# Splitting two GpSimd sums of the second half of the features, the first part ahead of the second matrix

## The chip, the cores and the metric

One core of one Trainium2 chip. The metric is the device time in microseconds of one execution of the whole program, median of several runs. The core's engines, as the profile names them: PE (TensorE, matrix products), PEld (its weight loads), DVE (VectorE), ACT (ScalarE), POOL (GpSimd), SP (SyncE, which issues most DMAs). Each engine works through its own queue of instructions in order; they wait for each other by semaphores.

## The reference

```python
# attention: batch 8, 8 heads, 576 positions, 64 wide; only the 32 best keys of a row count
scores = scale * np.matmul(q, k.transpose(0, 1, 3, 2))
kth = np.partition(scores, -32, axis=-1)[..., -32:-31]
scores = np.where(scores >= kth, scores, -1e9)
attn = softmax(scores)                    # in short
x = np.matmul(attn, v)                    # -> (4608, 512)
# feed-forward: 512 -> 2048 -> 512
h = x @ w_in
g = h - np.tanh(h)
out = g @ w_out
```

The softmax is written out in the reference, with the maximum of the row taken off and 1e-9 added to the sum.

## The kernel before

**Steps of attention.** A step is 128 rows of queries for one pair of heads (144 steps). Per step PE computes the scores (L350) into PSUM, ACT copies them out (L358), VectorE finds the 32nd largest value per row (L380 to L403: maxima of pairs, MAX8, match and replace), POOL makes from it a bias `tb` (L417) and `nb` (L426), ACT and POOL form the masked scores `z` (ACT L436, then POOL L439) and a check flag `bad` (POOL L443, for the step's two heads), ACT takes the exponential (L459), POOL adds the epsilon to its sum `rd` (L469), VectorE inverts it (L478), ACT multiplies (L485), VectorE transposes (L517), a DMA round trip sorts the blocks, and PE multiplies with the values (L582). Several steps are under way at once; in one round of the loop POOL gets, in this order, the z and flags of the last step, then `tb` and `nb` of the present one, then `rd` of the last.

**Feed-forward in units.** When 256 rows of x are complete they form a full unit (17 of them; two smaller units of 128 rows come first). A full unit is a list of 30 items of work, which are dealt out between the steps at a rate that a planner sets when the program is built. So the order on every engine is fixed in the program.

Items 0 to 15 (`ffn_full`, which calls `ffn_h`) form the features g = h - tanh(h), 128 of the 2048 features to an item. On every odd item ACT computes the tanh (L652) and copies h (L653), and POOL subtracts (L654). The features lie in two tiles `u.g[0]` and `u.g[1]`, "the first half" and "the second half" (index k), of four parts m = 0 to 3, each written by one odd item: items 9, 11, 13 and 15 write parts 0 to 3 of the second half.

Items of the product (`ffn_p`, 0 to 13) multiply g with the second matrix `w_out`. This is not done plainly but in Strassen's manner with seven products (`ORDER`), each in two items, k = 0 and 1. The tile of each half is split into four quarters, a11, a12, a21, a22 (`quarters`; in memory they lie in alternating blocks of 128 columns). The seven products take as left sides a11, a12, S2, S3, S1, a22 and S4, in this order, where the sums are, from `sum_up`:

- S1 = a21 + a22, into a buffer of its own (`sums[k]`, in the tile that the profile calls `et`)
- S3 = a21 - a11, in place of a21
- S2 = S1 - a11, in place of a11
- S4 = a12 - S2 (a11's place), in place of a12

POOL computes all of them, at L727, eight for each full unit. In the program each is put behind an item's matrix products. For the first half, S1 and S3 come in items 8 and 9 of the features. For the rest a table says behind which item of the product they come (first the half k, then the sum):

```python
SUMS = {
    0: [(1, "S1")],
    1: [(0, "S2"), (1, "S3")],
    2: [(1, "S2")],
    3: [(0, "S4")],
    4: [(1, "S4")],
}
```

PE's product items 0 and 1 read a11, items 2 and 3 a12, items 4 and 5 S2 of the first and second half, 6 and 7 S3, 8 and 9 S1, 10 and 11 a22, 12 and 13 S4. S2 may overwrite a11 once items 0 and 1 are through and S3 is formed. All of these products are at L626; `hx` and `hy` are the two accumulators. In the profile S2's products are the ones with `hx<-more,g` (first half) and `hx<-et,g` (second half), since their right sides lie in tiles of those names. The results are copied out by ACT (L786 to L803) and joined by POOL (L774).

Of the kernel before, what the change touches and what calls it, by code (L numbers as in the profile page):

```python
# [54 lines left out]
def kernel(  # L55
# [9 lines left out]
    nc = tc.nc  # L65
# [6 lines left out]
    S2 = S // 2  # L72
# [557 lines left out]
    def ffn_h(u, item):  # L630

        w = u.n
        per = 2 * P // w
        for f in range(item * per, (item + 1) * per):
            j, fo = f // FJ, (f % FJ) * P
            s = f * w % 512
            if s == 0:
                cur[u] = next_h("hps")
            for c in range(CD):
                (nc.tensor.matmul if per > 1 else by_columns)(  # L640
                    cur[u][:, s : s + w],
                    w_in[j][:, c, fo : fo + P],
                    u.xT[:, c, 0:w],
                    start=(c == 0),
                    stop=(c == CD - 1),
                )
        if item % 2:
            th = thpool.tile([P, 512], FP32, tag="th", name="th")
            if item % 8 == 1:
                u.g.append(gpool.tile([P, 4, 512], FP32, tag="g", name="g"))  # L650
            g = u.g[-1][:, item % 8 // 2, :]
            nc.scalar.activation(th[:], cur[u][:], AF.Tanh)  # L652
            nc.scalar.copy(g, cur[u][:])  # L653
            nc.gpsimd.tensor_tensor(g, g, th[:], ALU.subtract)  # L654
# [57 lines left out]
    def quarters(u, k):  # L712

        x = u.g[k][:].rearrange("p m (f t n) -> p m f t n", f=2, t=2)
        return [[x[:, :, f, t, :] for f in range(2)] for t in range(2)]

    def sum_up(u, k, x):

        (a11, a12), (a21, a22) = quarters(u, k)
        s1 = sums[k]  # L720
        out_, a, b, op = {
            "S1": (s1, a21, a22, ALU.add),
            "S3": (a21, a21, a11, ALU.subtract),
            "S2": (a11, s1, a11, ALU.subtract),
            "S4": (a12, a12, a11, ALU.subtract),
        }[x]
        nc.gpsimd.tensor_tensor(out_, a, b, op)  # L727

    ORDER = [("A11", "B11"), ("A12", "B21"), ("S2", "T2"), ("S3", "T3"), ("S1", "T1"), ("A22", "T4"), ("S4", "B22")]
    def bring(x):  # L730
# [4 lines left out]
    def product(u, i, k):  # L735
# [18 lines left out]
        return acc  # L754

    SUMS = {
        0: [(1, "S1")],
        1: [(0, "S2"), (1, "S3")],
        2: [(1, "S2")],
        3: [(0, "S4")],  # L760
        4: [(1, "S4")],
# [2 lines left out]
    def ffn_p(u, item):  # L764
# [11 lines left out]
        for x in SUMS.get(item, []):  # L776
            sum_up(u, *x)
# [32 lines left out]
    def combine_next():  # L810

        if combined[0] < len(COMBINE):
            x, j = COMBINE[combined[0]]
            if now[0] < (17 if x == "T3" else 20 if x in ("T2", "T4") else 0):
                return
            combine(x, j)
            combined[0] += 1
# [7 lines left out]
    def ffn_full(u, item):  # L825

        ffn_h(u, item)
        combine_next()
        if item in (8, 9):
            sum_up(u, 0, ("S1", "S3")[item - 8])  # L830

    def ffn(u):

        nh = CF * u.n // (2 * P)
        full = len(u.blocks) == 2
        for item in range(nh):
            f = (item + 1) * CF // nh - 1
            yield CD * (f // FJ + 1), u, lambda item=item: (ffn_full if full else ffn_h)(u, item)
        if not full:
            for part in range(CF // 2):  # L840
                yield CD * (WJ + part // 2 + 1), None, lambda part=part: ffn_small_o(u, part)
            return
        for item in range(2 * len(ORDER)):
            yield 2 * WJ * CD, None, lambda item=item: ffn_p(u, item)
# [277 lines left out]
```

## Time and profile before

| | us |
|---|---|
| median of 3 runs | 1488.9 (1487.57 to 1489.81) |
| the profiled execution | 1492.79 |
| its span, first to last instruction | 1489.7 |
| mean granted clock of PE | 0.971 |

The profile comes from one execution, and its instructions cover the span; about 3.1 us of that execution lie outside it.

| group (line, engine) | count | busy us | mean ns |
|---|---|---|---|
| sums L727 POOL, 128x512 | 136 | 174.4 | 1282 |
| differences g L654 POOL, 128x512 | 144 | 184.6 | 1282 |
| masked scores z L439 POOL, 128x576 | 288 | 405.3 | 1430 |
| joins L774 POOL, 128x256 | 51 | 37.4 | 734 |
| products with w_in L626 PE (`hps`) | 3840 | 438.9 | 384 |
| products with w_out L626 PE (`hx`, `hy`) | 2176 | 256.1 | 385 |

"Busy" is the time an engine had an instruction of that group under way; the 136 sums are the profile's three groups of that line added up. In 50 us stretches between 300 and 1250 us VectorE is busy for 47.6 to 49.9 us and PE for 45.1 to 50.0; from 1350 us on VectorE has almost nothing left to do and PE works off the remaining units.

### The profile page before, as it was taken

The page shows a single profiled execution, that of the slowest core. Times are in us where ns is not written, and L with a number is a line of the kernel's source. Part 1 is how long each engine was busy: PE and PEld are TensorE (multiplying, and loading weights), DVE is VectorE, ACT ScalarE, POOL GpSimd, SP SyncE. Part 2 cuts the span into 40 slices and gives each one's busy share as a digit, 9 for nine tenths or more (in the row PEclk, how much of TensorE's full clock was granted, in tenths as well). Part 3 has the DMA queues.
Part 4 walks back from the last instruction along what each step waited for, and adds up shares of the span by engine and source line. Part 5 has one row for each costly group of instructions (what it writes and reads, how often), then busy time and mean ns, then how long its engine had stood idle before and what let it go on. Part 6 is the DMA issues. An engine that isn't in the chain of part 4 may idle for free.

```text
span 1489.7 us, 35143 instructions
## 1 busy us (share of the span) xinstructions
PE 1378.2 (93%) x12036; PEld 881.8 (59%) x12036; DVE 1284.1 (86%) x4906; ACT 1031.8 (69%) x1922; POOL 1106.4 (74%) x1573
## 2 busy tenths in 40 slices
PE   4667899889999899999999999999999999999998
PEld 2455565556665555656666666666665666656665
DVE  7998988999999999999999999999999999883000
ACT  4776687778787777777687777777777777664321
POOL 3777679968788786968696969696978796866523
PEclk9787999999999999999999999999999999999999
DMA  9954101776776676676766767667666666643311
GB/s 258 359 206 169 55 21 64 187 198 164 194 181 185 162 189 176 173 191 153 180 152 192 177 175 183 182 162 195 167 179 176 170 163 190 155 129 110 105 32 46
DMA packets 241084, 242.25 MB, mean 163 GB/s; under 512 B 177408, under 2 KB 185600, under 8 KB 233728
## 3 DMA queue, kind: packets, MB, share of 16 engines
q1 hardware_dynamic: 239120, 239.69, 59.6%
q8 instruction: 98, 1.61, 0.5%
q14 instruction: 90, 0.74, 0.2%
q10 hardware_dynamic: 1776, 0.22, 0.1%
HBM read 153.99 MB, written 85.85 MB: 161 GB/s over the span
## 4 chain that ended last, share of the span: by engine, by line
PE 56%; DVE 25%; POOL 8%; DMA 5%; ACT 3%; issue 2%; SPq 1%; DVEq 0%; ACTq 0%; POOLq 0%
PE hps L626 23%; PE hx L626 10%; PE hy L626 7%; PE scps L350 6%; PE av L582 6%; DVE m L400 4%; DVE top L392 3%; DVE zx L517 3%; DVE rest L403 3%; POOL z L439 2%; POOL g L727 2%; DVE ab L386 2%; DVE top L403 1%; DVE ab L381 1%; PE hps L640 1%
## 5 line engine op out<-in xcount | busy, mean ns | idle before, releaser
L439 POOL TENSOR_TENSOR z<-sc,z 128x576 f32<-128x576 f32 x288 | 405.3, 1430 | 66.6 <-ACT z L436 66.2
L626 PE MATMUL hps<-xT,w_in 128*64 128x256 f32 x3840 | 438.9, 384 | 3.7 <-ACT g L653 3.6
L626 PEld LDWEIGHTS hps<-xT,w_in 128*64 128x64 f32 x3840 | 270.8, 138 | 162.9 <-issue 26.0
L654 POOL TENSOR_TENSOR g<-g,th 128x512 f32<-128x512 f32 x144 | 184.6, 1282 | 111.6 <-ACT g L653 110.3
L485 ACT ACTIVATE z<-z,rd 128x576 f32<-128x576 f32 x252 | 181.0, 766 | 80.4 <-DVE rd L478 78.5
L459 ACT ACTIVATE z<-z,nb 128x576 f32<-128x576 f32 x288 | 221.9, 775 | 16.5 <-POOL z L439 16.4
L436 ACT ACTIVATE z<-sc,tb 128x576 f32<-128x576 f32 x288 | 208.2, 775 | 27.6 <-POOL tb L417 23.9
L392 DVE MAX8 top<-ab 128x8 f32<-128x144 f32 x864 | 194.7, 295 | 0.0
L358 ACT COPY sc<-scps 128x1152 f32<-128x1152 f32 x144 | 160.9, 1118 | 47.8 <-PE scps L350 47.1
L517 DVE STREAM_TRANSPOSE zx<-z 128x1152 f32<-128x1152 f32 x126 | 171.6, 1362 | 24.1 <-ACT z L485 18.3
L350 PE MATMUL scps<-kT,qT 64*128 64x288 f32 (+1 forms) x1120 | 160.3, 435 | 28.4 <-DVE top L388 26.1
L400 DVE MAX8 m<-rest 128x8 f32<-128x168 f32 x576 | 161.6, 322 | 0.0
L400 DVE MAX8 m<-top 128x8 f32<-128x144 f32 (+1 forms) x576 | 152.8, 307 | 0.0
L350 PEld LDWEIGHTS scps<-kT,qT 64*128 64x128 f32 (+1 forms) x1120 | 87.4, 179 | 86.4 <-ACT z L436 26.6
L652 ACT ACTIVATE th<-hps 128x512 f32<-128x512 f32 x144 | 84.6, 587 | 75.3 <-PE hps L626 68.4
L626 PE MATMUL hx<-w_out,g 128*64 128x256 f32 x1088 | 130.7, 389 | 1.9 <-POOL g L654 1.9
L626 PE MATMUL hy<-more,g 128*64 128x256 f32 x1088 | 125.4, 381 | 0.0
L386 DVE TENSOR_TENSOR ab<-scps,sc 128x576 f32<-128x576 f32 x144 | 107.7, 748 | 0.0
L417 POOL TENSOR_SCALAR tb<-m 128x1 f32<-128x1 f32 x288 | 84.7, 304 | 29.7 <-DVE m L400 28.9
L626 PEld LDWEIGHTS hx<-w_out,g 128*64 128x64 f32 x1088 | 77.1, 139 | 48.8 <-issue 5.1
L626 PEld LDWEIGHTS hy<-more,g 128*64 128x64 f32 x1088 | 76.7, 137 | 43.0 <-issue 5.6
L443 POOL TENSOR_SCALAR bad<-top,tb 128x3 uint8<-128x3 f32 x288 | 97.5, 347 | 0.1
(126 smaller groups left out, 2350.9 us busy)
## 6 DMA issues: line engine op xcount, KB each, us to landing
there<-zx SPq DMA_DIRECT2D x56, 1152.0 KB, 4.9
spare<-there SPq DMA_DIRECT2D x224, 288.0 KB, 5.4
more<-kept_T SPq DMA_DIRECT2D x34, 512.0 KB, 3.8
out_dram<-ot SPq DMA_DIRECT2D x32, 256.0 KB, 2.9
there<-zx SPq DMA_DIRECT2D x14, 576.0 KB, 7.1
spare<-there SPq DMA_DIRECT2D x56, 144.0 KB, 3.2
vb<-in_v_dram SPq DMA_DIRECT2D x48, 128.0 KB, 5.4
kin<-in_k_dram SPq DMA_DIRECT2D x84, 72.0 KB, 4.4
```

The source lines that it names most:

```text
L350: nc.tensor.matmul(ps[rows, t, s, 0:S2], qT[g.b, g.hp + i, g.part][half(t), qs], kT[g.b, g.hp + i][half(t), ks], start=True, stop=True,)
L358: nc.scalar.copy(sc[:], ps[:, :, :, 0:S2])
L386: nc.vector.tensor_tensor(low[:, :, :, 0:W2], thirds(near), thirds(far), ALU.min)
L392: nc.vector.max(top[:, t, o : o + 8], low[:, t, i, :])
L400: nc.vector.max(m[:, t, m8], seen[i][t])
L436: nc.scalar.activation(zv[:, t, :], scf[:, t, :], AF.Relu, bias=tb[:, t : t + 1], scale=-BIG)
L439: nc.gpsimd.tensor_tensor(zv[:, t, :], scf[:, t, :], zv[:, t, :], ALU.subtract)
L459: nc.scalar.activation(x["zv"][:, t, :], x["zv"][:, t, :], AF.Exp, bias=x["nb"][:, t : t + 1], scale=scale, accum_out=den[:, t : t + 1],)
L485: nc.scalar.activation(x, x, AF.Copy, scale=rds[n][:, g.i, t : t + 1])
L517: nc.vector.transpose(tiles(zx, g.nq)[:, :, :, g.i, :].rearrange("p c k j -> p k c j"), z[:].rearrange("p (k c j) -> p k c j", c=NG, j=G),)
L626: nc.tensor.matmul(acc[half(t)], lhs[:, half(t)], rhs, start=start, stop=stop, skip_group_check=True)
L654: nc.gpsimd.tensor_tensor(g, g, th[:], ALU.subtract)
```

## The change

S1 and S3 of the second half are each formed in two instructions in place of one. `sum_up` gets an argument `ms`, the parts m that it covers. Parts 0 and 1 are summed behind items 12 and 13 of the features: S1 behind item 12 and S3 behind item 13, when items 9 and 11 have written those parts. Parts 2 and 3 are summed where the whole sum stood. All other sums stay whole and where they are.

```diff
-    def sum_up(u, k, x):
+    def sum_up(u, k, x, ms=slice(0, 4)):
...
-        nc.gpsimd.tensor_tensor(out_, a, b, op)
+        nc.gpsimd.tensor_tensor(out_[:, ms], a[:, ms], b[:, ms], op)
...
     SUMS = {
-        0: [(1, "S1")],
-        1: [(0, "S2"), (1, "S3")],
+        0: [(1, "S1", slice(2, 4))],
+        1: [(0, "S2"), (1, "S3", slice(2, 4))],
         2: [(1, "S2")],
         3: [(0, "S4")],
         4: [(1, "S4")],
...
         if item in (8, 9):
             sum_up(u, 0, ("S1", "S3")[item - 8])
+        if item in (12, 13):
+            sum_up(u, 1, ("S1", "S3")[item - 12], slice(0, 2))
```

The order of the instructions differs on POOL alone; on PE, VectorE, ACT and SP it is the same in both programs.

## The prediction

> **What bounds the kernel now.** I read four views, in this order: the busy times and the chain that ended last on the page, the groups of GpSimd's instructions kept apart by shape, the view of the sums' line with who waits for it, and then the timeline of each engine around all 17 full units.
>
> ```profile
> PE 1378.2 (93%) x12036; PEld 881.8 (59%) x12036; DVE 1284.1 (86%) x4906; ACT 1031.8 (69%) x1922; POOL 1106.4 (74%) x1573
> ...
> PE 56%; DVE 25%; POOL 8%; DMA 5%; ACT 3%; issue 2%; SPq 1%; DVEq 0%; ACTq 0%; POOLq 0%
> ```
>
> TensorE (PE) and VectorE (DVE) take turns as the bound; POOL is 74% busy and holds 8% of the chain. So a POOL instruction matters only where somebody stands waiting for it. Who waits for the sums is in the view of their line:
>
> ```profile
> who waited for it (us, times):
>   PEld hx L626: 13.6, 13
>   PE hx L626: 7.8, 8
> ```
>
> PE stands 7.8 us in all (its weight loads 13.6, in which the usual gap of some 0.4 before a load after another kind of matmul is included). What the queue looks like at such a place, here the unit at 705 us, first POOL and then PE:
>
> ```profile
> 692.53 0.23 POOL L469 TENSOR_SCALAR rd<-den 128x2 f32<-128x2 f32 x1 [0.66 <-ACT z L459]
> 694.56 1.29 POOL L654 TENSOR_TENSOR g<-g,th 128x512 f32<-128x512 f32 x1 [1.81 <-ACT g L653]
> ...
> 699.19 1.28 POOL L727 TENSOR_TENSOR et<-g 128x512 f32<-128x512 f32 x1
> 700.44 1.28 POOL L727 TENSOR_TENSOR g<-et,g 128x512 f32<-128x512 f32 x1
> 701.67 1.28 POOL L727 TENSOR_TENSOR g<-g 128x512 f32<-128x512 f32 x1
> 702.94 0.58 POOL L417 TENSOR_SCALAR tb<-m 128x1 f32<-128x1 f32 x2
> 703.49 0.25 POOL L426 TENSOR_SCALAR nb<-m 128x2 f32<-128x2 f32 x1
> 703.82 0.23 POOL L469 TENSOR_SCALAR rd<-den 128x2 f32<-128x2 f32 x1
> 704.13 1.28 POOL L727 TENSOR_TENSOR g<-et,g 128x512 f32<-128x512 f32 x1
> ```
>
> ```profile
> 705.46 1.95 PE L626 MATMUL hx<-et,g 128*64 128x256 f32 x16 [1.75 <-POOL g L727]
> ```
>
> The L727 rows are, in order, S1 of the second half, S2 of the first, S3 of the second and S2 of the second. The last is what PE waits for; S1 and S3 of the second half stand ahead of it, though PE wants S3 two product items later and S1 four. Ahead of 694.56 POOL had idled for 0.66 and 1.81 us. The queue is also late for others: VectorE's reciprocal and, through the flags' L443, its row L388 wait for POOL at
>
> ```profile
> 464.48 0.17 DVE L478 RECIPROCAL rd<-rd 128x2 f32<-128x2 f32 x1 [0.48 <-POOL rd L469]
> ...
> 633.05 0.17 DVE L478 RECIPROCAL rd<-rd 128x2 f32<-128x2 f32 x1 [0.47 <-POOL rd L469]
> ...
> 1218.38 0.45 DVE L388 TENSOR_TENSOR top<-ab,scps 128x288 f32<-128x288 f32 x1 [0.95 <-POOL bad L443]
> ```
>
> **What the Trainium skill says.** "GPSIMD Engine Reference", section 2.1, puts a dispatch cost on every instruction and a two-input floor of about 2.5 cycles an element. The trace agrees in form: 456 ns for 128x128 (L600), 734 for 128x256 (L774), 1282 for 128x512, which is 275 ns for each 128 columns and some 180 fixed; splitting a sum pays the fixed part twice. "Perfetto Trace Analysis", section "GPSIMD Engine Instruction", wants spacings of starts rather than durations; here 1.24 between sums against 1.28 reported, and 0.69 after L774. "SBUF — State Buffer", section "SBUF: two separate sides", has GpSimd and VectorE block each other on shared ports; the 136 sums take 1268 to 1312 ns whatever VectorE does, so I put no price on that. "Perfetto Trace Analysis", section "Optimization Strategy", says to find the gaps of the bounding engine and what ends them, which is what the sum below does.
>
> **The change part by part.**
>
> *Added:* per full unit two half sums: S1's after item 12, S3's after item 13. Each costs 0.70 us of queue (L774's shape, same bytes; the strided full-size rows cost no more than the contiguous ones, 1283 against 1280, so bounds of 0.65 and 0.75). *Removed:* half of S1 at product item 0 and of S3 at item 1: 1.24 - 0.70 = 0.54 each. Net on POOL: 2 x (0.70 - 0.54) = 0.32 a unit, x 17 = 5.4 us of 1106. No DMA, no queue of SP or ACT and no matmul moves. The order of POOL around the new pieces, as the two programs have it: L654 of item 11, half S1, [z, flags of the step], L654 of 13, half S3, [tb, nb, rd], L654 of 15; where a step boundary falls differs from unit to unit. Neither half waits for another engine: what each reads was written by POOL's own L654 before.
>
> *What the added halves delay.* I walked POOL's queue through each unit: later by 0.70 at each new half, less each idle gap, minus 0.54 at each shortened sum. The delay on the way peaks at 1.3 to 1.4 just after the second half. Behind it are L654 of items 13 and 15 (PE's first product), z (L439; ACT's exponential waits), tb (ACT's mask) and rd (VectorE's reciprocal). Cover, from the consumers' starts in the trace: rd has 1.4 to 4.2 us of slack against at most 1.3; z 0.67 at the tightest against 0.70; tb 1.2 to 4.4 against 1.4, with the exception of the unit at 1062 (0.19), where ACT then idles 2.56 us before its next instruction, so 1.2 is swallowed there. L654 of item 15 mostly waits for ACT after idle gaps of 0.56 to 2.19. In the units at 773 and 846 it does not, and arrives 1.32 late at 773.2 and 845.6; PE wants this last quarter some 3.2 us into the product, at 773.5 and 846.3. So I price the delays at 0, with 0.3 at each of these two as the other bound, and 2 us in all if the cover of tb and z is thinner than it looks.
>
> *What the shortened sums advance.* At the first half's S2 POOL is 0.54 earlier, less delay left; from the second half's S2 on 1.08, less delay left. By the walk the advance there is 1.05 to 1.08 in the units around 378, 455, 543, 624, 705, 1067, 1212 and 1285, 0.94 at 1142, 0.54 at 782, and 0.4 to 0.75 at 850, 922 and 994. What that is worth is the smaller of advance and wait, where the wait is on the chain:
> - 464.5: reciprocal 0.48.
> - 624 to 633: reciprocal twice 0.47, together 0.94.
> - 705: PE waits 1.75, so 1.08; VectorE, next on the chain, idles 2.16 for these scores.
> - 782: PE waits 1.58, advance 0.54.
> - 1142: PE waits 1.47, advance 0.94.
> - 1218: L388 waits 0.95 behind POOL's flags, and PE's scores 1.83 behind L388: 0.95.
> - 1282 and 1285: PE waits 0.29 and 0.65: 0.94.
>
> Together 5.87 us. Worth nothing: the unit at 543 (PE waits 1.75, but VectorE and DMA carry the chain there until 570, where PE waits for VectorE again), those at 295, 378, 850, 922, 994 and 1067 (PE or VectorE busy throughout) and the three in the last 150 us, where PE is the bound and waits for none of the sums. From this I take 1.0: dependent neighbours on POOL show gaps of 0.08, and with two more such neighbours a unit the advance is some 0.15 smaller at seven places. Result: 4.9 us.
>
> Against the profiled execution: 1492.8 (span 1489.7 and 3.1 around it) - 4.9 = 1487.9. The median shown is 3.9 below that execution, so the forecast for it is 1488.9 - 4.9 = 1484.0. What would be late next: at 705 and 1142 PE still waits 0.5 to 0.7 for the same S2, at 782 1.0; at the other places VectorE or PE itself.
>
> **The rivals.**
> - *The time goes into another wait.* PE and VectorE alternate, and VectorE is at 95 to 100% in most of the 50 us stretches from 300 to 1250; what PE gains at 705, 782 or 1142 it could spend at its next scores, waiting for L388, as it does at 570. For it: 26.1 us of such waits in 12 places. Against: after 782 PE runs 190 us without a break, after 1142 67 us, while VectorE idles. If only those two and 1285 hold half their value: 1.2 us, so 1487.7.
> - *The extra pieces come at the wrong place: slower.* The place is items 12 to 15, where tb, rd and L654 stand behind up to 1.4 us of new work. It decides once POOL's idle gap before item 15's L654 is gone, as at 773 and 846 already: then PE's product waits about 0.7 (1.4 less half of it in the ACT wait) in 12 of the 14 units ahead of the tail, 8.4 us, against which the gains above still count for 4: 1493.3. For it: two units without a gap, tb slacks of 1.2 and less. Against: 12 of the 14 have a gap of 0.56 and more, seven of them over 1.
> - *It doesn't do what it says.* If the tracking of overlaps made PE's first product wait for the half S3 (interleaved columns of the same tile), that half would still precede item 15's L654 in POOL's order, for which PE waits anyway: no time, and the kinds of waits on PE are the same in both programs. I give this no chance of its own.
>
> **How the numbers follow.** Forecast, 1482 to 1485.9: 0.57. Still better by luck of the new alignment, about 1480: 0.03. Time moved to other waits, 1486 to 1491.8: 0.27. Slower, 1492 to 1496: 0.13. A measurement here can tell about 0.2% (3 us) from nothing; so faster 0.60, same 0.27, slower 0.13. Range with 2 in 10 left out: 1481.5 to 1490.5; the forecast's own is 1482 to 1485.9.
>
> **What would show it.** Rows of L727 with 128x256, 68 of them near 0.73 us, POOL busier by some 5 us; PE's waits for L727 down from 7.8 to about 3; the 0.47 and 0.48 waits of the reciprocal gone; no new waits of PE for L654 (1.9 us now) or of ACT for tb (23.9). Wrong if these waits shrink while PE's waits for L388 (26.1) grow as much, or if L654's grow.

## The result and the profile after

| | before | after |
|---|---|---|
| median of 6 runs each, us | 1489.4 (1487.6 to 1490.6) | 1482.9 (1481.0 to 1484.6) |
| ratio after to before | | 0.9955 (0.9945 to 0.9965) |
| the profiled execution / its span, us | 1492.8 / 1489.7 | 1481.0 / 1479.2 |

The change takes off 6.5 us, between 5.2 and 8.2 by the interval. The forecast was a gain of 4.9 us and a time of 1484.0.

A part of the 6.5 us lies outside the profile. In the kernel before, some 3.3 us of an execution lie outside the span of its instructions (3.1 in the profiled one); in the kernel after it is 1.8, and so it is in every kernel of the experiments below, also in those that gain nothing. These 1.4 us are thus not the work of the earlier sums. Where they come from is open. Between the first and the last instruction the change takes off some 5 us.

The busy times and the chain that ended last, from the page of the kernel after:

```profile
PE 1371.2 (93%) x12036; PEld 876.7 (59%) x12036; DVE 1281.5 (87%) x4906; ACT 1030.9 (70%) x1922; POOL 1113.0 (75%) x1607
...
PE 44%; DVE 35%; POOL 9%; DMA 5%; ACT 4%; issue 2%; SPq 1%; DVEq 0%; ACTq 0%; POOLq 0%
```

POOL has 34 instructions more and is busy 6.6 us longer (1106.4 before). The shares of the chain are not a verdict: a second profile of the same kernel gave PE 52%, DVE 29%, POOL 6%. PE and VectorE are so close to each other that small shifts pass the chain from one to the other.

GpSimd's groups of line 727 in the kernel after, shapes kept apart (busy us, mean ns of one, then the idle time of POOL just before them):

```profile
L727 POOL TENSOR_TENSOR g<-g 128x256 f32<-128x256 f32 x34 | 25.0, 736 | 0.0
L727 POOL TENSOR_TENSOR et<-g 128x256 f32<-128x256 f32 x34 | 25.0, 735 | 1.7
```

68 half sums of 0.735 us. Who waits for that line, in the kernel after:

```profile
who waited for it (us, times):
  PEld hx L626: 7.4, 9
  PE hx L626: 3.8, 4
```

PE stood 7.8 us for the sums before, and stands 3.8 now. The view of all waits of the kernel after (total us, times, longest) has the other queues that the prediction spoke of:

```profile
PE scps L350 <- DVE top L388: 29.8, 14, 5.3
...
ACT z L436 <- POOL tb L417: 20.0, 15, 3.6
...
ACT z L459 <- POOL z L439: 12.9, 21, 2.2
...
DVE rd L478 <- POOL rd L469: 8.3, 4, 3.1
```

VectorE's wait for `rd` went from 12.9 to 8.3 us, ACT's for `tb` from 23.9 to 20.0 and for `z` from 16.4 to 12.9: these three came no later in sum. PE's wait for the last part of the second half's features (L654) grew from 1.9 to 2.5, and that of its weight loads from 3.7 to 5.8; growth there was one of the prediction's signs of being wrong. The kernel of the ten other units below has 2.6 and 5.6 and is no slower for it, so no time can be seen in it. PE's wait for VectorE's L388 is 3.7 us longer here than before, which the prediction had named as the sign of a rival. In the second profile of the change it is 25.5, below the 26.1 of before: it varies with the execution and says nothing on the change.

The unit that the prediction had shown, now at 696. First POOL, then PE (start, duration, engine and line, in brackets the idle time before and its releaser):

```profile
683.03 1.27 POOL L654 TENSOR_TENSOR g<-g,th 128x512 f32<-128x512 f32 x1
684.27 0.73 POOL L727 TENSOR_TENSOR g<-g 128x256 f32<-128x256 f32 x1
684.99 0.58 POOL L417 TENSOR_SCALAR tb<-m 128x1 f32<-128x1 f32 x2
...
686.17 1.29 POOL L654 TENSOR_TENSOR g<-g,th 128x512 f32<-128x512 f32 x1
...
690.80 0.73 POOL L727 TENSOR_TENSOR et<-g 128x256 f32<-128x256 f32 x1
691.49 1.28 POOL L727 TENSOR_TENSOR g<-et,g 128x512 f32<-128x512 f32 x1
692.74 0.73 POOL L727 TENSOR_TENSOR g<-g 128x256 f32<-128x256 f32 x1
...
694.64 1.27 POOL L727 TENSOR_TENSOR g<-et,g 128x512 f32<-128x512 f32 x1
```

```profile
695.97 1.95 PE L626 MATMUL hx<-et,g 128*64 128x256 f32 x16 [1.04 <-POOL g L727]
```

Before, POOL idled for 0.66 and 1.81 us ahead of the last L654; now neither idle gap is there, and that time holds the half sums. From 690.80 the three sums ahead of `tb` take 2.66 us up to 693.46, where they had taken 3.75 before (699.19 to 702.94). PE's wait is 1.04 in place of 1.75.

**How much of the two profiles' difference is the change's.** The spans differ by 10.5 us, but 3.8 of these are there at 250 us, before the first full unit. And PE's granted clock falls to half for 3.4 or 6.8 us now and then (a dip, below), and not at all the same places in each execution. Stretches of the kernel after (PE busy, number of matmuls, granted clock, DMA share, GB/s):

```profile
1310.00:1315.00 5.00, 2.67 (x24) 0.95 0.00 0
1315.00:1320.00 5.00, 5.00 (x32) 0.71 0.58 239
```

and the same work in the kernel before:

```profile
1322.00:1327.00 5.00, 2.67 (x26) 1.00 0.00 0
1327.00:1332.00 5.00, 5.00 (x44) 1.00 0.58 236
```

The dip at 1314 costs the kernel after 1.6 us. So a ledger, the gain listed place by place, is only to be had between two executions whose dips lie alike; the experiments gave such a pair.

### The profile page after: what moved, and what is told of

Same layout as the page of the kernel before. It is cut to its first block, busy times and chain, and to the rows that moved or that the text cites. A ratio compares the mean times of both kernels' runs of the same rounds, so it can differ in the third digit from the quotient of the medians.

```text
span 1479.2 us, 35177 instructions
## 1 busy us (share of the span) xinstructions
PE 1371.2 (93%) x12036; PEld 876.7 (59%) x12036; DVE 1281.5 (87%) x4906; ACT 1030.9 (70%) x1922; POOL 1113.0 (75%) x1607
## 4 chain that ended last, share of the span: by engine, by line
PE 44%; DVE 35%; POOL 9%; DMA 5%; ACT 4%; issue 2%; SPq 1%; DVEq 0%; ACTq 0%; POOLq 0%
PE hps L626 17%; PE hx L626 8%; PE hy L626 6%; DVE m L400 6%; PE scps L350 5%; PE av L582 5%; DVE top L392 5%; DVE zx L517 4%; DVE rest L403 4%; DVE ab L386 3%; POOL z L439 3%; DVE top L403 2%; DVE ab L381 2%; POOL g L654 2%; DVE scps L380 2%
## 5 line engine op out<-in xcount | busy, mean ns | idle before, releaser
L654 POOL TENSOR_TENSOR g<-g,th 128x512 f32<-128x512 f32 x144 | 184.5, 1282 | 93.6 <-ACT g L653 91.8
L459 ACT ACTIVATE z<-z,nb 128x576 f32<-128x576 f32 x288 | 222.0, 777 | 13.0 <-POOL z L439 12.9
L358 ACT COPY sc<-scps 128x1152 f32<-128x1152 f32 x144 | 161.1, 1118 | 49.9 <-PE scps L350 49.4
```

The source lines that it names most:

```text
L358: nc.scalar.copy(sc[:], ps[:, :, :, 0:S2])
L459: nc.scalar.activation(x["zv"][:, t, :], x["zv"][:, t, :], AF.Exp, bias=x["nb"][:, t : t + 1], scale=scale, accum_out=den[:, t : t + 1],)
```

## The experiments

The theory of the prediction: the gain arises at seven places, where somebody waits for POOL on the chain, as large as the smaller of wait and advance there; the added pieces cost nothing, since they lie in idle gaps of POOL. Against it stand that the gain is spread over all units or comes from a new alignment of the whole schedule, and that short pieces help as such, wherever they stand. Each ratio below is to the kernel before, run on the same chip; 0.1% is 1.5 us. Each also holds the 1.4 us from outside the instructions, so a kernel that changes nothing inside them comes out near 0.999. The diffs are against the kernel after.

**Only the seven units, and only the other ten.** Units are counted from 0; those at 464, 624, 705, 782, 1142, 1218 and 1285 us are 2, 4, 5, 6, 11, 12 and 13. In the other units the sums stay whole and late. The diff is that of the seven; the second kernel has `AHEAD = (0, 1, 3, 7, 8, 9, 10, 14, 15, 16)`.

```diff
+    AHEAD = (2, 4, 5, 6, 11, 12, 13)
...
-            sum_up(u, *x)
+            sum_up(u, *(x if u.no in AHEAD else x[:2]))
...
-        if item in (12, 13):
+        if item in (12, 13) and u.no in AHEAD:
```

> The early halves are made only in the seven full units (of 17, counted from 0: 2, 4, 5, 6, 11, 12, 13) in which the forecast found somebody waiting on the chain; in the other ten both sums stay whole. Theory 1 (an earlier S2 is worth time only where PE or VectorE stand waiting for GpSimd's queue): the whole gain of the change, 5 to 7 us less than before, ratio 0.9953 to 0.9967. Theory 2 (each unit's burst is eased by about the same, 6.5 us over 17 units): 7/17 of it, 2.7 us, ratio 0.998. Theory 3 (two shorter instructions fit the queue better, wherever they stand): as theory 2, about 2.7 us.

> The early halves are made only in the other ten full units (0, 1, 3, 7, 8, 9, 10, 14, 15, 16). Theory 1: nothing, within 1.5 us of before, ratio 0.999 to 1.001. Theories 2 and 3: 10/17 of 6.5 us, 3.8 us less, ratio 0.9975.

Measured: the seven 1481.8, ratio 0.9944 (0.993 to 0.9959); the other ten 1488.8, ratio 0.9993 (0.9985 to 1.0002). By the medians of the spans alone the seven are 6.7 us shorter than before (1480.0 against 1486.7) and the ten 0.3 longer (1487.0). So the gain inside the instructions arises in the seven units that were picked from the trace of before, and ten times the same two pieces elsewhere are worth nothing and cost nothing that can be measured. The 8.3 us of the seven by the ratio (6.1 to 10.4) lie above the 5 to 7 that were expected; whether they beat the whole change (5.2 to 8.2) is not told apart.

**Both parts at the old place.** The sums are split, but nothing comes earlier.

```diff
-        0: [(1, "S1", slice(2, 4))],
-        1: [(0, "S2"), (1, "S3", slice(2, 4))],
+        0: [(1, "S1", slice(0, 2)), (1, "S1", slice(2, 4))],
+        1: [(0, "S2"), (1, "S3", slice(0, 2)), (1, "S3", slice(2, 4))],
...
-        if item in (12, 13):
-            sum_up(u, 1, ("S1", "S3")[item - 12], slice(0, 2))
```

> S1 and S3 of the second half are split into two instructions as in the change, but both parts stand where the whole sum stood, in all 17 units. Theory 1: no advance, and S2 of the second half is 0.32 us later (two sums of 1.24 us become four of 0.70): 0 to 2.2 us slower than before, ratio 1.000 to 1.0015. Theory 2: the burst is longer, not shorter, 0.3 us in each unit: as theory 1 or up to 5 us slower, ratio to 1.0035. Theory 3: faster than before by much of the 6.5 us, ratio under 0.998.

Measured: 1490.7, ratio 1.0 (0.9987 to 1.0012). From the waits of this kernel:

```profile
DVE rd L478 <- POOL rd L469: 14.3, 12, 4.3
PE hx L626 <- POOL g L727: 9.6, 10, 1.9
```

Short pieces alone make the waits for POOL longer (12.9 and 7.8 before). The equal time hides this, since 1.4 us are gone outside the instructions: the medians of the spans are 1488.9 here and 1486.7 before. It is the place that brings the gain.

**Another order of the sums, none split.** With S3 formed first, S2 is S3 + a22, and neither sum needs S1; S1 = a11 + S2 and S4 = a12 - S2 are wanted only several products later. So what PE waits for needs two sums of the second half in place of three. The seven left sides are the same; S1 and S2 are added up in another order of their terms. S2 now lies in the buffer that S1 had, and S1 in place of a11.

```diff
-        s1 = sums[k]
+        s2 = sums[k]
...
-            "S1": (s1, a21, a22, ALU.add),
+            "S1": (a11, a11, s2, ALU.add),
             "S3": (a21, a21, a11, ALU.subtract),
-            "S2": (a11, s1, a11, ALU.subtract),
-            "S4": (a12, a12, a11, ALU.subtract),
+            "S2": (s2, a21, a22, ALU.add),
+            "S4": (a12, a12, s2, ALU.subtract),
...
-        lhs = {"A11": a11, "A12": a12, "A22": a22, "S1": sums[k], "S2": a11, "S3": a21, "S4": a12}[left]
+        lhs = {"A11": a11, "A12": a12, "A22": a22, "S1": a11, "S2": sums[k], "S3": a21, "S4": a12}[left]
...
-        0: [(1, "S1", slice(2, 4))],
-        1: [(0, "S2"), (1, "S3", slice(2, 4))],
-        2: [(1, "S2")],
-        3: [(0, "S4")],
-        4: [(1, "S4")],
+        0: [(1, "S3")],
+        1: [(1, "S2")],
+        4: [(0, "S1")],
+        5: [(1, "S1")],
+        6: [(0, "S4")],
+        7: [(1, "S4")],
...
-            sum_up(u, 0, ("S1", "S3")[item - 8])
-        if item in (12, 13):
-            sum_up(u, 1, ("S1", "S3")[item - 12], slice(0, 2))
+            sum_up(u, 0, ("S3", "S2")[item - 8])
```

> No sum is split. The same eight sums per unit are formed in another order: S3 = a21 - a11 in place, then S2 = S3 + a22 into the buffer that S1 had, so that S2 needs neither S1 nor PE's first product; S1 = a11 + S2 in place of a11, later (behind product items 4 and 5), S4 = a12 - S2 behind items 6 and 7. Both sums of the first half stand behind feature items 8 and 9. What precedes the second half's S2 shrinks from four whole sums to two, and S1 and S4 leave the burst. Theory 1: every wait of PE for S2 goes, also the 0.8 to 1.2 us that are left in the changed kernel at the units near 696, 773 and 1132 us, so 8 to 11 us less than before, ratio 0.9925 to 0.9947. Theory 2: like the change or a little more, about 6 to 10 us. Theory 3: nothing, since no instruction is shorter: ratio 0.999 to 1.001.

Measured: 1478.4, ratio 0.9928 (0.9911 to 0.9944): 11.5 us under the kernel before by the medians, 10.7 by the ratio (8.3 to 13.3), and better than the change. Who waits for the sums' line in this kernel, and then PE and POOL at the same unit:

```profile
who waited for it (us, times):
  PEld hx L626: 0.4, 1
```

```profile
695.56 1.90 PE L626 MATMUL hx<-more,et 128*64 128x256 f32 x16
697.28 1.90 PE L626 MATMUL hx<-et 128*64 128x256 f32 x16
```

```profile
693.32 1.29 POOL L727 TENSOR_TENSOR g<-g 128x512 f32<-128x512 f32 x1
694.69 1.27 POOL L727 TENSOR_TENSOR et<-g 128x512 f32<-128x512 f32 x1
695.95 0.59 POOL L417 TENSOR_SCALAR tb<-m 128x1 f32<-128x1 f32 x2
```

S2 is there at 695.96 (694.69 and 1.27), 1.3 us ahead of PE at 697.28. No matmul waits for a sum any more, ACT's wait for `tb` falls to 11.6 us, and POOL has no instruction more than before. These four kernels settle where the change's gain inside the instructions comes from, and this one shows that it took about half of what lay there (6.5 of 11.5 us, or some 5 of 10 without the 1.4 from outside).

**One piece at a time, and four units.** S1's first part alone ahead; S3's first part alone; both, but only in units 5, 6, 11 and 13, where PE itself waits. With S3 alone, S1 reads parts of a21 after S3 has replaced them, so this kernel's output is not that of the reference, and only its time is used. The first two were run twice, since S3 alone came out at first as good as both, and the second time the change stood beside them.

```diff
-        1: [(0, "S2"), (1, "S3", slice(2, 4))],
+        1: [(0, "S2"), (1, "S3")],
...
-        if item in (12, 13):
-            sum_up(u, 1, ("S1", "S3")[item - 12], slice(0, 2))
+        if item == 12:
+            sum_up(u, 1, "S1", slice(0, 2))
```

> Only S1 of the second half has its first part behind feature item 12; S3 stays one sum where it was. Theory 1: the second half's S2 is 0.54 us earlier instead of 1.08; at each of the seven places the smaller of 0.54 and the wait counts (0.48, 0.54, 0.54, 0.54, 0.54, 0.54, 0.54 us), 3.7 us less than before, ratio 0.9975. Theory 2 (the burst is eased): half of the change, 3.3 us. If the whole gain hung on S3 (the only one of the two that stands between S2 of the first and of the second half): nothing, ratio 1.000.

> Only S3 of the second half has its first part behind feature item 13; S1 stays one sum where it was. It therefore reads parts 0 and 1 of a21 after S3 has replaced them, which changes the values of S1 and not its time. Theory 1: again 0.54 us of advance, now for the second half's S2 alone and not for the first half's, 3 to 3.7 us less than before, ratio 0.9975 to 0.998. If the whole gain hung on S1: nothing.

> The early halves are made only in the four full units (5, 6, 11, 13) in which PE itself waits for S2. Theory 1: 1.08 + 0.54 + 0.94 + 0.94 = 3.5 us less than before, ratio 0.9976; what the seven units gave beyond that is then the part at which VectorE waits for tb, rd or the flags (units 2, 4, 12: 2.4 us). Theory 2 (all units alike): 4/17 of 6.5, 1.5 us, ratio 0.999.

> The kernel with only S1's first part early, again, on the same chip as the next two. Read on the traces place by place, the gains of S1 alone and of S3 alone were each near 3.7 us; their medians were 5.1 and 6.4 us under before, which would mean that either half brings nearly all of the change. Theory 1 with the advance counted (0.54 us at each of seven places): 3.7 us under before, ratio 0.9975, and the change ahead of it by 2 us or more. If one half is enough (a wait only has to fall under some bound): the same as the change, 0.9955.

> The kernel with only S3's first part early, again (S1 reads parts 0 and 1 of a21 after S3 has replaced them: other values of S1, the same time). Theory 1 with the advance counted: 0.9975, with half a microsecond more from the other units at most, 0.997. If one half is enough: 0.9955.

> The changed kernel itself, beside the two kernels with one half each. Theory 1 with the advance counted: 5.9 to 6.5 us under before, ratio 0.9955 to 0.996, and 2 us or more ahead of either half alone. If one half is enough: no difference between the three.

| | ratio | interval |
|---|---|---|
| S1 alone | 0.9966 | 0.9953 to 0.9979 |
| S1 alone, again | 0.9971 | 0.996 to 0.9982 |
| S3 alone | 0.9957 | 0.9942 to 0.9971 |
| S3 alone, again | 0.9971 | 0.9962 to 0.9981 |
| the change, again | 0.9959 | 0.9943 to 0.9975 |
| units 5, 6, 11, 13 | 0.9979 | 0.9968 to 0.9989 |

S3's first value lay below what was expected; the second, 0.9971, about where it was then expected. In the second pair each piece alone takes off some 4.3 us (0.29%), the change 6.1: a lead of 1.8 us, where 2 or more was expected, and not clear of the intervals. The traces tell them apart. Read at the seven places like the table in the next section, S1 alone gives 3.4 us, S3 alone 3.5 and the change 5.7. That the halves sum to more than the whole fits the theory: one piece advances the queue by 0.54 us, which is about the size of the smaller waits, so that seven places give 7 x 0.53 = 3.7, and the second piece finds something left only where the wait is longer.

The four units give 3.1 us (1.6 to 4.8), of which 1.4 lie outside the instructions; the terms of the prediction for them sum to 3.5. Their trace, against that of the ten units, shows 3.2 us at these four places, but their runs scatter from 1481.9 to 1491.4, so the times don't confirm the 3.5. Nor do they confirm the other three units, where VectorE waits: expected were 2.4 us, the traces show 2.5, and the difference of the two ratios is 5.2 with an uncertainty of about as much as the surplus.

**How thin the cover is.** The first part of S1 is formed two or three times over, with the same data each time. This delays everything behind it by 0.8 or 1.6 us a unit and changes nothing else. The diff is that of three times.

```diff
-            sum_up(u, 1, ("S1", "S3")[item - 12], slice(0, 2))
+            for _ in range(3 if item == 12 else 1):
+                sum_up(u, 1, ("S1", "S3")[item - 12], slice(0, 2))
```

> As the change, but the first part of S1 behind feature item 12 is formed three times over, so that 1.4 us more of GpSimd's work stands ahead of the second half's last two differences in every unit; nothing behind them changes. Theory 1 with the queue walked on the trace of before: where GpSimd idles ahead of the last difference the extra work is swallowed (units at 705, 1212, 1285: the advance stays 0.5 to 0.8), where it does not, S2 comes later than before (units at 624, 782 and 1142 by 0.2, 0.9 and 0.3) and the last difference late for PE (units at 773, 846 and 983, about 1 us each). Sum: gains of 2.4 against losses of 3 to 4, so from 1 us less to 4 us more than before, ratio 0.9993 to 1.0027. If what stands ahead of the differences is always covered: as the change, 0.9955. If it is never covered: 1.4 us in each of 14 units, 20 us less the change's 6.5, ratio 1.009.

> As the change, but S1's first part is formed twice over, 0.8 us more of GpSimd's work ahead of the second half's last differences in every unit. Three times over (1.6 us more) had cost 17.7 us against the change, some 0.8 of the 1.6 us in each of 14 units. If the cover ends just at the change's own delay and every further microsecond counts alike: half of that, 8.8 us more than the change, ratio 1.0014. If some cover is left beyond the change's 1.4 us: clearly less, 2 to 5 us more than the change, ratio 0.997 to 0.999.

Measured: three times 1499.9, ratio 1.0074 (1.0057 to 1.0091); twice 1487.6, ratio 0.9985 (0.9979 to 0.9992). Three times was expected at most 0.27% above the kernel before and lies far outside, nearer to the 1.009 for no cover at all. Twice lies where it was expected if some cover is left. The waits of this kernel:

```profile
ACT z L436 <- POOL tb L417: 28.1, 22, 3.6
...
ACT z L459 <- POOL z L439: 22.4, 36, 2.8
...
DVE rd L478 <- POOL rd L469: 17.4, 18, 3.1
...
PE hx L626 <- POOL g L654: 12.5, 10, 2.4
```

and one of its units, POOL and then PE:

```profile
764.94 2.35 POOL L727 TENSOR_TENSOR et<-g 128x256 f32<-128x256 f32 x3
767.25 1.27 POOL L654 TENSOR_TENSOR g<-g,th 128x512 f32<-128x512 f32 x1
768.49 0.73 POOL L727 TENSOR_TENSOR g<-g 128x256 f32<-128x256 f32 x1
...
772.59 1.26 POOL L654 TENSOR_TENSOR g<-g,th 128x512 f32<-128x512 f32 x1
```

```profile
769.32 3.24 PE L626 MATMUL hx<-w_out,g 128*64 128x256 f32 x28
773.90 0.65 PE L626 MATMUL hx<-w_out,g 128*64 128x256 f32 x4 [1.34 <-POOL g L654]
```

PE has done 28 of the 32 matmuls of the first product and stands 1.34 us for the last part of the second half's features, the L654 of item 15, which the pieces hold up. Such waits are 2.5 us in the change, 6.2 with one more piece and 12.5 with two. In time, by the ratios to before: the change's own pieces lie in the gaps; 0.8 us more a unit costs 3.9 us (0.9985 - 0.9959), 0.3 on average for each of the 14 units that have steps beside them; the next 0.8 costs 13 us (1.0074 - 0.9985), 0.9 a unit, so all of it. This is the place and the mechanism of the prediction's slower rival, at a larger delay.

## Why the prediction was right

The time lay 1.1 us under the forecast, inside its own narrow range. That is closer than the prediction can claim for itself: 1.4 us of the gain lie outside the instructions, which no step of it had in view. What it forecast, 4.9 us inside them, is to be set against some 5 us by the times. The second profile of the change and that of the ten other units have their dips of the clock alike, but for one at 643 that is longer in the change. So the gain at each place can be read from the starts of the score copies (ACT, L358) on either side of it, change less ten units:

| place | predicted, us | measured, us |
|---|---|---|
| 464, reciprocal | 0.48 | 0.59 |
| 624 to 633, reciprocal twice | 0.94 | 0.92 |
| 705, PE waits for S2 | 1.08 | 1.08 |
| 782, PE waits for S2 | 0.54 | 0.33 |
| 1142, PE waits for S2 | 0.94 | 0.70 |
| 1218, L388 behind the flags | 0.95 | 1.02 |
| 1285, PE twice | 0.94 | 1.07 |
| together | 5.87 | 5.71 |

Between these places the difference moves by some tenths and comes back, but for 1.3 us lost around 646 to the longer dip and 0.3 lost between 795 and 1130. At 705 the score copies give 1.28, but ACT itself was 0.2 late with the copy before; the table has the 1.08 of PE's own starts. First the ten units, then the change:

```profile
692.49 3.67 PE L626 MATMUL hy<-w_out,g 128*64 128x256 f32 x32
696.33 1.95 PE L626 MATMUL hx<-more,g 128*64 128x256 f32 x16 [0.17 <-POOL g L727]
700.00 1.95 PE L626 MATMUL hx<-et,g 128*64 128x256 f32 x16 [1.73 <-POOL g L727]
```

```profile
692.95 3.67 PE L626 MATMUL hy<-w_out,g 128*64 128x256 f32 x32
696.45 1.90 PE L626 MATMUL hx<-more,g 128*64 128x256 f32 x16
699.38 1.95 PE L626 MATMUL hx<-et,g 128*64 128x256 f32 x16 [1.03 <-POOL g L727]
```

From the first to the last of these starts it is 7.51 us and 6.43: 0.34 are gained at S2 of the first half and 0.74 at that of the second. So PE's remaining wait shrank by less than the gain because a part was gained one product earlier.

- *The ledger of seven places:* right as a sum to 0.2 us. The single terms are off by up to 0.24 to both sides, so a part of the closeness of the sum is luck.
- *The deduction of 1.0 us:* by the ledger this term was mis-sized. It was taken for dependent neighbours on POOL, as 0.15 less advance at seven places. Such a loss is seen at 782 and 1142 (0.21 and 0.24), but not at the other five; together the seven places lost 0.2 us and not 1.0. The total time can't decide it. Without the deduction the forecast would have been 1483.0, against 1482.9 measured, but that closeness is luck, since 1.4 us of the measured gain come from outside the ledger. What is left, 3.8 to 6.8 us by the interval, holds 4.9 and 5.9 both.
- *PE's waits for the sums down to about 3:* 3.8. At 705, 782 and 1142 there remain 1.04, 1.24 and 0.77 where 0.67, 1.04 and 0.53 were worked out.
- *The reciprocal's waits:* of 0.48, 0.47 and 0.47 one of 0.13 is left, at 627.
- *POOL busier by 5.4:* 6.6. The 5.4 was reckoned in spacings of starts (0.70 and 1.24), the page counts durations: 4 x 0.735 less 2 x 1.28 is 0.38 a unit, 6.5 in 17.
- *The added delays at 0, bounds up to 2 us:* right for the change as far as the time shows, since the ten units are no slower; PE's waits for L654 did grow a little (1.9 to 2.5). The cover ends right there, though: the two kernels with more pieces show that the next 0.8 us is already partly paid for and the one after it wholly.
- *The rival in which the time goes to PE's waits for L388:* not seen; 26.1 before, 29.8 and 25.5 in two profiles of the change, while the time was gained in both. (PE's run without a break after 1142 is 75 us in the trace of before, not 67; the argument is the same.)
- *The slower rival:* its mechanism exists, but its point lies some 0.8 us of delay further on than the change goes.

That the advance at 543 is worth nothing was right too (that unit is among the ten).

## What to carry to other kernels

Count a change on a shared in-order engine by places: at each, the smaller of what the instruction comes earlier and what somebody on the chain stands waiting there; everything else was worth nothing here, and the sum held to 0.2 us. Work moved into an engine's idle gaps is free only up to the size of the gaps: here 1.4 us was free, 0.8 more cost 0.3 a unit, and the next 0.8 cost all of itself. And before splitting what is late, ask whether the late thing needs it: with S2 formed without S1, no sum was split and the gain was 11.5 us in place of 6.5.

## What was not expected of the hardware

- Behind the first 160 us, the granted clock of PE dips to half for 3.4 or 6.8 us five to seven times before the last few us of an execution (at 263, 314, 485, 564 and 1314 us in the profile after). The dips follow PE's own pauses: in all 14 profiles each of them begins during or shortly behind an idle stretch of PE of 1.8 to 5.3 us. The pauses near 485 and 565 us (3.4 to 4.8 us) have a dip behind them in every profile; those near 315, 645 and 1320 us (3.1 to 3.4, 3.0 to 3.6 and 2.3 us) only in some. So shorter waits of PE may also save a dip; no run here separates that. One of 3.4 us at a place where PE bounds costs 1.6 us, more than the gain at any single place here (1.08).
- Two executions differed by 3.8 us before the first instruction that the change touches. Of a difference of 10.5 us between two spans some 6 were the change's.
- The kernel before has 3.3 us of its time outside its instructions, and every other kernel here 1.8. A difference of times is to be held against the difference of spans before it is explained by what the trace shows.
